# One core, adaLN with a Fourier mixer and an MLP: the modulation's first two vectors loaded scale first, the shift added inside the folds, and a planner that counts the half clock

## The chip, the core and the metric

The program runs on one core of one Trainium2 chip. The core has five engines that run their own instruction streams and meet through semaphores: TensorE (PE, matrix products; its weight loads are listed apart as PEld), VectorE (DVE), ScalarE (ACT), GpSimd (POOL) and SyncE (SP, which here only issues DMA transfers). Data lie in the DRAM of the device and in the core's SBUF (128 partitions); products land in PSUM, eight banks of 128 x 512 fp32 numbers. The metric is the device time of the whole program in microseconds (us). The kernel before the change takes 1337.07 us, the median of three runs (1335.74 to 1341.33).

## The reference

Sequence length 2048, width 1024, hidden width 3584, batch 1, all fp32. The core of it:

```python
x = A_x
mod = (_silu(c) @ w_mod).reshape(c.shape[0], 6, 1, -1)
sa, ca, ga, sb, cb, gb = (mod[:, 0], mod[:, 1], mod[:, 2], mod[:, 3], mod[:, 4], mod[:, 5])
h = _layernorm(x, axis=-1) * (1 + ca) + sa
x = x + ga * _A_ref(h, ...)      # real part of DFT_seq(DFT_hidden(h)), by four DFT matrices
h = _layernorm(x, axis=-1) * (1 + cb) + sb
x = x + gb * _B_ref(h, B_w1, B_b1, B_w2, B_b2)   # layernorm, w1 and b1, tanh gelu, w2 and b2
```

So there are two halves: a Fourier mixing of the modulated x, and an MLP on the modulated result. Six vectors of 1024 numbers, the modulation, come out of one product of silu(c) with the 1024 x 6144 matrix w_mod. The first two, the shift sa and the scale 1+ca, are needed at the start.

## The kernel before, in words

**Precision.** Products that need fp32 results run in fp16: each operand is scaled by a power of two and split into a high and a low half, and three products are summed (high x high, high x low, low x high).

**The front, up to about 305 us of the trace.** Four groups of work overlap there.

1. *Loads and the modulation.* SP issues the loads in an order written out in the code: rows of x (x0 to x15, 128 rows of 1024 each), a quarter of w1, and the first 2048 columns of w_mod (sa and ca together) as eight loads of 1 MB, one for each 128 rows k (`wm2(k)`). `mod_part(k)` (line 2604) multiplies silu(c) with each in fp32, four quarters of 512 columns, on 32 partitions each. When the last k is done, `row_max` (line 2615) and an all-reduce on POOL give the largest absolute value of sa and ca, `scales` makes a power of two of it, `rows_out` (2628) and `cols` (2633) turn the vectors into columns, and `cols_out` (2637 to 2645) writes `mcol` (scaled columns), `mneg` and `mbias`. All of it together is the task "mod".
2. *First layernorm and even/odd folds.* A cosine transform needs only sums and differences of mirrored columns, so the normalised x is folded. x comes in four groups bt = 0..3 of four tiles. For each group: statistics on DVE (line 2693) for bt 0 to 2 and on ACT for bt 3, the normalisation on ACT (2723 to 2727), transposes on PE (2740), then per pair of transposed blocks one ACT instruction with scale and shift (2753, task `lna`) and two DVE instructions (2757 and 2758, task `lnd`) that add and subtract the mirrored block. Groups 0 and 1 make class 0, groups 2 and 3 class 1. For each class `folds` then adds and subtracts further (2808 twice, 2814 twice, 2827 four times), and each of its two halves, called hop, is split by ACT (2833, high) and DVE (2835, low).
3. *Hidden and sequence transforms.* `hid` units (2.1 us each in the plan, line 3060) multiply the hops with DFT columns: class 0's products, then class 1's. Their results are split by ACT (2586) and DVE (2589). Eight blocks b = 0..7 of the sequence transform follow; in each, Q (3136) then P (3124) on PE, a copy on ACT (3140), and two DVE adds that form y (3145 and 3150, task `yev`).
4. *Second layernorm and z.* For each block: ga times y (3267), x added by a DMA, sums of squares on ACT (3241, 3615), cb and sb applied on DVE (3296, 3300), normalisation (3309); then the result is transposed (3490, `zT`), combined by unit products (3498), and split into seven sums z (3511 on ACT, 3538 on DVE) for the MLP's products. The z of blocks 4 to 7 are stored to DRAM by POOL (3530), behind which stand its other transfers (2183, 3271). Blocks 6 and 7 are held: their z is made later, during the main products.

Beside this, DVE and ACT split the first parts of w1 and w2 and the DFT matrices (2434, 2447, 2461, 2586, 2589), and the other modulation vectors are made row by row (2956, 2969).

**The main products.** gemm3 (line 3962) and gemm4 (line 4089), 2352 matmuls each, work by a scheme with seven products in place of eight. The first two groups of gemm3 need only z of blocks 0 to 3. They begin at about 275 us, and from about 305 us to the end PE runs them back to back.

**What sets the order.** A planner in the program's own Python: every piece of work is a `Task` with an engine, a cost in us, and the tasks it needs. Tasks wait in streams, each with an urgency `due` (smaller goes first). `pick_first` lets the engine that is free earliest take the most urgent task that can start. Costs, lags after a dependency (`LAGS`) and landing times (`LANDS`) are constants. The plan fixes the order in which each engine's instructions are written; on the chip each engine then runs its own in that order and waits where it must. `due_at(v)` says when the held blocks' z is made among the main products.

## Time and profile before

| | us |
|---|---|
| median of three runs | 1337.07 (1335.74 to 1341.33) |
| profiled execution | 1336.37 |
| its span, first to last instruction | 1334.6 |
| start of the first hidden product (line 3060) | 107.33 |
| start of the first main product (line 3962) | 274.91 |
| from where the main products run without a gap | 305.04 |
| last of PE's work | 1324.8 |
| mean granted TensorE clock | 0.964 |

PE is busy for 92% of the span, DVE for 79%, ACT for 56%, POOL for 19%. Over the main products PE is busy 1012.77 of 1019.80 us; before that it is busy 215.74 of 305 us. A "granted clock" of 0.5 means that the TensorE clock ran at half of full speed in that stretch. In a row of the timeline the bracket at the end gives how long the engine had been idle before that group of instructions and what ended the wait; in a table of windows each line is start:end, length, and the busy time of PE, PEld, DVE, ACT and POOL with the number of instructions, then the granted clock, the DMA engines' busy share and GB/s.

### The profile page before, as it was taken

Reading aid. Unit: us, or ns where it says so; the run is one execution under the profiler, and the core shown is the slowest. Engines: PE = TensorE matmul, PEld = TensorE weight load, DVE = VectorE, ACT = ScalarE, POOL = GpSimd, SP = SyncE. Lnnn points to the kernel's source line nnn. Section 1 sums busy time; section 2 is a strip of 40 time slices with the busy share of each in tenths; the row PEclk is TensorE's granted clock in tenths of the full one; section 3 lists DMA queues with packets and bytes.
Section 4 is the critical chain, followed back from the end, with each engine's and each line's share of the span. In section 5 each row is a group of like instructions: output and inputs, shape, how many; then the busy total and the mean of one; then the engine's idle time right before and its main releaser. Section 6 shows DMA issues by size and latency. Waiting matters only on the chain.

```text
span 1334.6 us, 16823 instructions
## 1 busy us (share of the span) xinstructions
...
## 2 busy tenths in 40 slices
...
GB/s 364 402 298 268 111 244 214 173 262 278 170 113 231 107 247 175 196 156 111 251 89 291 162 394 170 292 271 331 200 298 176 270 240 190 199 280 195 60 177 114
DMA packets 105704, 292.59 MB, mean 219 GB/s; under 512 B 13340, under 2 KB 13356, under 8 KB 103688
## 3 DMA queue, kind: packets, MB, share of 16 engines
...
## 4 chain that ended last, share of the span: by engine, by line
PE 69%; DVE 6%; issue 2%; ACT 2%; DMA 1%; POOL 0%; SPq 0%; DVEq 0%; POOLq 0%
PE ps L3962 34%; PE ps L4089 34%; DVE arena L2447 2%; DVE arena L4141 1%; ACT arena L2434 1%; DMA fw<-arena 1%; DVE arena L2461 1%; DVE arena L3538 0%; DVE arena L3988 0%; ACT arena L3981 0%; PE ps L3387 0%; ACT arena L3511 0%; DVE arena L3296 0%; DVE arena L3375 0%; DVE arena L4196 0%
## 5 line engine op out<-in xcount | busy, mean ns | idle before, releaser
L3962 PE MATMUL ps<-arena 128*128 128x512 f16 x2352 | 514.6, 381 | 7.8 <-DVE arena L3150 6.6
L4089 PE MATMUL ps<-arena 128*128 128x512 f16 x2352 | 511.7, 379 | 5.9 <-DVE arena L4141 5.4
L3962 PEld LDWEIGHTS <-arena 128*128 128x128 f16 x2352 | 231.0, 98 | 287.9 <-issue 13.2
L4089 PEld LDWEIGHTS <-arena 128*128 128x128 f16 x2352 | 230.0, 98 | 284.4 <-issue 7.6
L4141 DVE SCALAR_TENSOR_TENSOR arena<-ps,i4c,arena 128x1024 f32<-128x1024 f32 x179 | 229.2, 1280 | 79.5 <-PE ps L4089 78.3
L2434 ACT ACTIVATE arena<-arena,shc 128x512 f16<-128x512 f32 (+1 forms) x115 | 116.2, 1016 | 119.4 <-DVE arena L2461 67.0
L2447 DVE SCALAR_TENSOR_TENSOR arena<-arena,shc 128x512 f16<-128x512 f32 (+1 forms) x115 | 128.9, 1121 | 39.1 <-ACT arena L2434 38.9
L3846 ACT ACTIVATE arena<-arena 128x512 f32<-128x512 f32 (+4 forms) x159 | 97.3, 613 | 111.7 <-DVE arena L3855 91.1
L2461 DVE TENSOR_TENSOR arena<-arena 128x512 f32<-128x512 f32 (+1 forms) x196 | 149.4, 764 | 4.0
L3981 ACT ACTIVATE arena<-arena,b1s,i1c 128x512 f32<-128x512 f32 x78 | 63.4, 813 | 86.4 <-DVE arena L3988 86.4
L2434 ACT ACTIVATE arena<-arena,s1c 128x512 f16<-128x512 f32 (+1 forms) x70 | 60.6, 886 | 65.2 <-DVE arena L2461 33.5
L3855 DVE TENSOR_TENSOR arena<-arena 128x256 f32<-128x256 f32 x240 | 88.4, 419 | 3.6 <-DMA arena<-in_cre_dram 3.0
L3988 DVE TENSOR_TENSOR arena<-arena,ps 128x512 f32<-128x512 f32 x78 | 53.3, 684 | 43.2 <-PE ps L3962 41.9
L3627 POOL PARTITION_ALL_REDUCE sums<-sums x21 | 11.5, 552 | 373.3 <-DVE sums L3623 355.2
L2447 DVE SCALAR_TENSOR_TENSOR arena<-arena,s1c 128x512 f16<-128x512 f32 (+1 forms) x70 | 65.9, 960 | 10.0 <-ACT arena L2434 9.6
L3984 ACT ACTIVATE arena<-ps 128x512 f32<-128x512 f32 x78 | 45.9, 589 | 39.0 <-PE ps L3962 38.7
L2447 DVE SCALAR_TENSOR_TENSOR arena<-arena,s2c 128x1024 f16<-128x1024 f32 x49 | 61.7, 1279 | 2.9 <-ACT arena L2434 2.8
L2434 ACT ACTIVATE arena<-arena,s2c 128x1024 f16<-128x1024 f32 x49 | 54.7, 1137 | 2.7 <-DVE arena L2461 1.7
L3060 PE MATMUL ps<-arena 128*128 128x256 f16 (+5 forms) x297 | 47.0, 310 | 8.3 <-ACT arena L2833 3.2
L3615 ACT ACTIVATE ps<-arena 128x1024 f32<-128x1024 f32 x46 | 46.8, 1018 | 9.1 <-DMA arena<-in_w_dram 4.7
L3892 POOL DMA_DIRECT2D arena<-in_cim_dram x69 | 38.1, 558 | 54.6 <-ACT arena L3846 26.4
L2740 PE MATMUL ps<-ident,arena 128*128 128x128 f32 x128 | 23.3, 329 | 25.1 <-POOL arena L2901 14.7
...
## 6 DMA issues: line engine op xcount, KB each, us to landing
...
```

What stands on the lines that cost most here:

```text
L2434: act.activation(o[m][0], q(j), AF.Copy, **sc)
L2447: dve.scalar_tensor_tensor(o[m][1], q(j), scale, o[m][0], op0=ALU.mult, op1=ALU.subtract)
L2461: dve.tensor_tensor(q(d), q(a), q(b), op=op)
L3060: pe.matmul(PA(bp + o, (1, w), pn=m), l, r, start=i == 0, stop=i == len(mm_) - 1)
L3615: act.activation(junk, parts[j][0], AF.Square, accum_out=t[:, j : j + 1])
L3846: f = lambda: act.activation(v, v, AF.Square, accum_out=csum[0:pn, n : n + 1])
L3855: return lambda: dve.tensor_tensor(dst[0][:, o::2], src[0][:, o::2], dst[0][:, o::2], op=op)
L3962: pe.matmul(ps.rearrange("p (k t) -> p k t", k=4), w1at(g, m)[:, a, d * P : (d + 1) * P], zc(m)[:, b, :, d, :], start=(start and d == 0 an ...
L3981: act.activation(dst, src, AF.Gelu_apprx_tanh, scale=inv, bias=b1s[:, 2 * p + j : 2 * p + j + 1])
L3988: after_pe("dve", 0.6, lambda: dve.tensor_tensor(q, q, ps[b], op=ALU.add), kp[b])
L4089: pe.matmul(t[:, j], hidc[:, c_, m, a, k * P : (k + 1) * P], w2c[:, m, c_, w], start=(start and c_ == 0 and n == 0), stop=(c_ == 1 and n = ...
L4141: lambda: dve.scalar_tensor_tensor(dst, ps[b], inv, dst, op0=ALU.mult, op1=ALU.add), kp[b],
```

## The change

Four things are changed together. Line numbers from here on that belong to the changed program are some 80 to 110 higher than those of the kernel before.

**1. The two modulation vectors in two halves.** The eight 1 MB loads become sixteen of 0.5 MB: the scale half (ca) for all k before x8 to x11, the shift half (sa) behind them, into the same eight buffers (each waits for the scale half's product of its k). `mod_part`, `rows_out`, `cols` and `cols_out` run once for each half; the scale half ends in "moda", the shift half in "mod". The columns are no longer multiplied by the common power of two: the split into high and low (line 2833's and 2835's places) does that instead.

```diff
-    for i in range(4):
-        load_x(i)
+    def load_wm(h):
+        for k in range(8):
+            f = lambda k=k: sp.dma_start(wm2(k), wm[:, k, h * D : (h + 1) * D])
+            load(("wm", h, k), f, [] if h else [("mp", 1, k)])
...
-    for i in range(4, 8):
-        load_x(i)
-    for k in range(8):
-        load(("wm", k), lambda k=k: sp.dma_start(wm2(k), wm[:, k, 0 : 2 * D]), cost=2.75)
-    for i in range(8, 12):
-        load_x(i)
+    load_xs(1)
+    load_wm(1)
+    load_xs(2)
+    load_wm(0)
+    load_draw()
...
-    def cols_out():
-        dve.tensor_scalar(
-            mcol.rearrange("p a (b r) c -> p (a b) (r c)", b=2), PA(TB_, (32, 4), (128, 4)), sh, None, op0=ALU.mult
-        )
+    def cols_out(h):
+        dve.tensor_copy(mcol[:, h].rearrange("p (b r) c -> p b (r c)", b=2), PA(TB_ + 64 * h, (32, 2), (128, 4)))
+        if h:
+            dve.tensor_scalar(mneg, mcol[:, 1, 2:4], -1.0, None, op0=ALU.mult)
+            return
...
+        add("modr", "act", 0.66, lambda h=h: rows_out(h), [last_mp], ("rowc", h), 1.0)
+        add("modp", "pe", 0.6, lambda h=h: cols(h), [("rowc", h), *([] if h else ["vspec", "moda"])], ("cols", h), 1.0)
+        add("modm", "dve", 0.3 if h else 0.9, lambda h=h: cols_out(h), [("cols", h), *([] if h else ["sh"])], "moda" if h else "mod", 1.0)
```

**2. The shift of class 0 in the folds.** For class 0 `lna` multiplies by the scale alone and needs only "moda". The shift is constant along the sequence, so it is added after the first folds, in `s2_bias`: four instructions of 128 x 256, one of 128 x 1024 and two tiny ones in place of one `s2` of 128 x 2048. Class 1 stays as it was and needs "mod".

```diff
-                k1 = add("lna", "act", 0.78, lambda e=e, ba=ba, sc=sc, bi=bi: act.activation(
-                    e, bank(ba), AF.Identity, scale=sc, bias=bi), [ks[0], "mod"], None, 1.6)
+                if cls:
+                    f = lambda e=e, ba=ba, sc=sc, bi=bi: act.activation(e, bank(ba), AF.Identity, scale=sc, bias=bi)
+                else:
+                    f = lambda e=e, ba=ba, sc=sc: act.activation(e, bank(ba), AF.Copy, scale=sc)
+                k1 = add("lna", "act", 0.78, f, [ks[0], "mod" if cls else "moda"], None, 1.6)
...
-        k1 = add(f"fold{cls}", "dve", 2.4, lambda: s2(0, ALU.add), [k1], None, due)
+        def s2_bias():
+            for j in range(2):
+                for arr in range(2):
+                    o = FA(eo(j, arr, 0, 0), (1, 256))
+                    dve.scalar_tensor_tensor(
+                        o, o, mbias4[:, arr, j : j + 1], FA(eo(j, arr, 0, 512), (-1, 256)), op0=ALU.add, op1=ALU.add
+                    )
+            o = FA(eo(0, 2, 0, 0), (4 * AR, 2), (AR, 2), (1, 256))
+            dve.tensor_tensor(o, o, FA(eo(0, 2, 0, 512), (4 * AR, 2), (AR, 2), (-1, 256)), op=ALU.add)
+            o = [FA(eo(j, 0, 0, 0), (AR, 2), (256, 2)) for j in range(2)]
+            for j in range(2):
+                dve.tensor_tensor(o[j], o[j], medge[:, j], op=ALU.add)
+
+        if cls:
+            k1 = add(f"fold{cls}", "dve", 2.4, lambda: s2(0, ALU.add), [k1], None, due)
+        else:
+            k1 = add(f"fold{cls}", "dve", 3.0, s2_bias, [k1, "mod"], None, due)
...
-            h = add(f"foldh{cls}", "act", 2.0, lambda hi=hi, src=src: act.activation(hi, src, AF.Copy), [ka, *(([("n", 15), ("wrr", 5)] + [("cru", 6), ("cru", 7)] * loc) if cls else [("wrr", 2)])], None, due)
+            h = add(f"foldh{cls}", "act", 2.0, lambda hi=hi, src=src: act.activation(hi, src, AF.Copy, scale=sh), [ka, "mod", *(([("n", 15), ("wrr", 5)] + [("cru", 6), ("cru", 7)] * loc) if cls else [("wrr", 2)])], None, due)
             add(
-                f"foldl{cls}", "dve", 2.4, lambda hi=hi, lo=lo, src=src: dve.tensor_tensor(lo, src, hi, op=ALU.subtract),
+                f"foldl{cls}", "dve", 2.4, lambda hi=hi, lo=lo, src=src: dve.scalar_tensor_tensor(lo, src, sh, hi, op0=ALU.mult, op1=ALU.subtract),
```

**3. A plan with a half clock, and unused products.** In the front the planner now models the TensorE clock in windows of 3.41 us (`pe_run`): a window with little PE work makes a later one run at half speed. Where a planned PE task would start after a gap, and from 45 us of the plan on, `keep_warm` writes products of the identity matrix (128 x 128 fp16, 256 columns) into a PSUM bank that is free then. Nothing reads them. There are 129 of them in the changed program: 7 ahead of the last transposes of the layernorm, one among class 1's hidden products, and the others in groups of 3 to 23 from the sequence transform on.

```diff
+            if self.eng == "pe" and in_order[0]:
+                keep_warm(self, self.start())
             t = self.start() + self.cost
+            if self.eng == "pe" and in_order[0]:
+                t = pe_run(self.start(), self.cost, 0.7 if self.tag == "hidp" else 1.0)
...
+    TICK, PHASE = 3.4133, 0.0
+    pe_work, pe_state = {}, [0.5]
...
+    def pe_run(t, cost, weight):
+
+        while cost > 1e-9:
+            k = int((t - PHASE) // TICK) + 1
+            while len(pe_state) <= k:
+                w = pe_work.get(len(pe_state) - 1, 0.0) / TICK
+                n = len(pe_state)
+                up = w > 0.85 or min(pe_work.get(n - i, 0.0) for i in (1, 2, 3)) > 0.6 * TICK
+                pe_state.append(0.5 if w < 0.46 else 1.0 if up else pe_state[-1])
+            d = min(cost / pe_state[k], PHASE + k * TICK - t + 1e-6)
+            pe_work[k] = pe_work.get(k, 0.0) + weight * d
+            cost -= d * pe_state[k]
+            t += d
+            pe_spans.append((t - d, t))
+        return t
+
...
+    def keep_warm(task, start):
+
...
+        free = dict(spare)
+        if task.own:
+            free[task.own[0]] = max([0.0] + [done[d] + LAT for d in task.own[1] if d is not None])
+        b = min(free, key=lambda k: free[k])
+        idle = TICK - sum(e - max(s, start - TICK) for s, e in pe_spans)
+        n = int(min(start - max(clk["pe"], free[b]) - 0.3, idle - IDLE) / 0.11)
+        if n <= 0:
+            return
+        w = ident.bitcast(F16) if hasattr(ident, "bitcast") else ident[:, :].bitcast(F16)
+        for _ in range(n):
+            pe.matmul(PA(512 * b, (1, 256)), w[:, 0:P], w[:, 0 : 2 * P], start=True, stop=True)
+        clk["pe"] = pe_run(max(clk["pe"], free[b]), 0.11 * n, 1.0)
...
+    KEEP, IDLE = 45.0, 0.8
```

**4. Urgencies, costs and places.** A table `DUES` of 59 entries replaces the urgency of named streams, and some costs, lags and addresses change with it. The held blocks' z moves: its first transposes stand behind main product 972 instead of 696, those of the second behind 1716 instead of 1500. The steps' arithmetic stays the same.

```diff
+    DUES = {
+        ("cop0l", 58.0): 63.7, ("cop0l", 59.0): 60.5, ("cop1l", 61.0): 58.9, ("coph", 26.0): 40.3,
...
+    }
...
+            t.tag, t.due, t.lag = tag, DUES.get((stream, due), due), LAGS.get(f"{stream}l" if t.eng == "dma" else stream, LAGS.get(stream, LAT))
             streams.setdefault(f"st_{stream}" if t.eng == "st" else stream, deque()).append(t)
...
-    LAGS = {"w": 2.0, "rowl": 1.0, "crawl": 0.5, "row": 0.2, "rowp": 3.0, "ld": 0.5, "z": 1.0, "s": 0.5, "u": 0.3, "op": 0.4, "comb": 0.3, "ln": 0.2}
+    LAGS = {"w": 2.0, "rowl": 1.0, "crawl": 0.5, "row": 0.2, "rowp": 0.4, "ld": 0.5, "z": 1.0, "s": 0.5, "u": 0.3, "op": 0.4, "comb": 0.3, "ln": 0.2}
...
-        return due[3, 2] + 200.0 + 150.0 * v
+        return due[3, 2] + 150.0 + 180.0 * v
```

What this does to the order is seen in three places. **The first** is DVE between about 40 and 60 us of the trace, where the modulation's columns are made and the folds begin. Before (line 2615 is the largest value, 2637 to 2645 the columns, 2757 and 2758 the folds):

```order
L2447 SCALAR_TENSOR_TENSOR arena_65<-arena_65,s1c_171 128x2x512
L2615 TENSOR_REDUCE mx_121<-ps 128x1
L2619 TENSOR_SCALAR vspec_122<-ps,sel_123 128x2 x2
L2622 TENSOR_SCALAR m_4_109<-mx_121 128x1
...
L2637 TENSOR_SCALAR mcol_124<-ps,m_4_109 128x16
L2640 TENSOR_SCALAR msp_125<-ps,m_4_109 4x2
L2641 TENSOR_SCALAR mneg_126<-mcol_124 128x4
L2642 TENSOR_TENSOR mbias_127<-mcol_124 128x2
...
L2589 SCALAR_TENSOR_TENSOR arena_65<-arena_65 128x2x257
L2757 SCALAR_TENSOR_TENSOR arena_65<-ps,mneg_126,arena_65 128x512
L2758 SCALAR_TENSOR_TENSOR arena_65<-ps,mcol_124,arena_65 128x512
```

Now (2720 and 2722 write the columns, 2850 and 2851 are the folds, 2783 statistics, 2695 the largest value):

```order
L2720 COPY mcol_124<-ps 128x8
L2722 TENSOR_SCALAR mneg_126<-mcol_124 128x4
L2517 SCALAR_TENSOR_TENSOR arena_65<-arena_65,s1c_172 128x2x512
L2850 SCALAR_TENSOR_TENSOR arena_65<-ps,mneg_126,arena_65 128x512
L2851 SCALAR_TENSOR_TENSOR arena_65<-ps,mcol_124,arena_65 128x512
...
L2783 BN_STATS xst_22_165<-arena_65 128x6 x2
...
L2695 TENSOR_REDUCE mx_121<-ps 128x1
...
L2901 TENSOR_TENSOR arena_65<-arena_65 128x2x2x512 x2
L2907 TENSOR_TENSOR arena_65<-arena_65 128x8x256
L2699 TENSOR_SCALAR vspec_122<-ps,sel_123 128x2 x2
...
L2917 SCALAR_TENSOR_TENSOR arena_65<-arena_65,vspec_122 128x256 x4
```

The first fold stands right behind the scale's columns; all eight pairs of class 0, the statistics of group 2 and three of the large folds stand ahead of the columns of the shift.

**The second** is DVE around the last y of the sequence transform (3145 and 3150 before, 3256 and 3261 now; the rows between are ln2 of blocks 4 and 5 and the splits of z). Before:

```order
L3296 SCALAR_TENSOR_TENSOR arena_65<-arena_65,lns_25_167 128x1024
L3538 TENSOR_TENSOR arena_65<-ps,arena_65 128x2x512
L2673 RECIPROCAL lns_24_166<-lns_24_166 128x2
...
L3300 SCALAR_TENSOR_TENSOR arena_65,lns_24_166<-arena_65,lns_24_166 128x1024 x2
L3296 SCALAR_TENSOR_TENSOR arena_65<-arena_65,lns_25_167 128x1024
L3288 SCALAR_TENSOR_TENSOR csum_160<-csum_160 128x2
L3145 TENSOR_TENSOR arena_65<-ps,arena_65 128x2x256
L3150 TENSOR_TENSOR arena_65<-ps,arena_65 128x2x257
```

Now (3378 is what 3267 was, 3649 what 3538 was):

```order
L3649 TENSOR_TENSOR arena_65<-ps,arena_65 128x2x512
L2763 RECIPROCAL lns_24_167<-lns_24_167 128x2
...
L3418 SCALAR_TENSOR_TENSOR lns_24_167<-lns_24_167 128x2
L3378 SCALAR_TENSOR_TENSOR arena_65,lns_25_168<-arena_65 128x1024
L3399 SCALAR_TENSOR_TENSOR lns_25_168<-lns_25_168,csum_161 128x2
L3256 TENSOR_TENSOR arena_65<-ps,arena_65 128x2x256
L3649 TENSOR_TENSOR arena_65<-ps,arena_65 128x2x512
L3378 SCALAR_TENSOR_TENSOR arena_65,csum_161<-arena_65 128x1024
L3261 TENSOR_TENSOR arena_65<-ps,arena_65 128x2x257
```

The two passes of 3300 and the passes of 3296 no longer stand between the last two y; two large instructions now stand between the halves of the last y.

**The third** is POOL's queue of transfers at the end of the front (3530 before and 3641 now store z of block 4, then of block 5; 3271 and 3382 add a held block's row tile to the output; 3627 and 3738 are the all-reduce for the scale of w2). Before:

```order
L3530 DMA fzc_68<-arena_65 256x1x512
L2183 DMA out_dram<-arena_65,idxm_108 1024x1024
L3530 DMA fzc_72<-arena_65 256x1x512
L3530 DMA fzc_70<-arena_65 256x1x512
L3271 DMA out_dram<-arena_65 128x1024
L3530 DMA fzc_71<-arena_65 256x1x512
L3530 DMA fzc_73<-arena_65 256x1x512
L3530 DMA fzc_69<-arena_65 256x1x512
L3627 ISA sums_2032<-sums_2032 128x1
L3530 DMA fzc_67<-arena_65 256x1x512
```

Now:

```order
L3641 DMA fzc_71<-arena_65 256x1x512
L3382 DMA out_dram<-arena_65 128x1024
L3641 DMA fzc_73<-arena_65 256x1x512
L3641 DMA fzc_69<-arena_65 256x1x512
L2183 DMA out_dram<-arena_65,idxm_108 1024x1024
L3382 DMA out_dram<-arena_65 128x1024
L3641 DMA fzc_67<-arena_65 256x1x512
L3738 ISA sums_2182<-sums_2182 128x1
L3641 DMA fzc_68<-arena_65 256x1x512
```

All seven stores of block 4 are now issued ahead of the second held block's output transfers and ahead of the all-reduce. On PE, at the same place, 24 main products stand ahead of block 5's transposes before (12 of them ahead of block 4's); now it is 72 (12 and then 60), all behind block 4's transposes, ahead of which 25 of the unused products stand.

137 lines of the change are left out of this document (87 added, 50 removed), and 3 rows, old and new, of the table DUES.

## The prediction, made before the changed kernel was run

> **What bounds the kernel now.** I read the table by stretches first, then the timeline at each border of it, then the rows of single costs. The stretches end at the first product of the modulation's columns, the columns' end, the first hidden product, class 1's long run of hidden products, the last hidden result, the first main product, the point from which those run without a gap, and PE's end. Columns: start:end, length, busy PE, PEld, DVE, ACT, POOL, granted clock, DMA share, GB/s.
>
> ```profile
> 20.30:46.70 26.40, 18.00 (x89) 4.91 (x88) 11.21 (x34) 13.23 (x25) 3.73 (x7) 0.75 1.02 417
> 46.70:107.30 60.60, 39.68 (x206) 20.92 (x206) 55.43 (x85) 50.60 (x81) 0.35 (x1) 0.80 0.96 323
> 107.30:139.10 31.80, 25.37 (x200) 14.09 (x199) 29.07 (x33) 17.59 (x25) 1.71 (x2) 0.95 0.64 228
> 139.10:169.30 30.20, 28.32 (x138) 14.52 (x139) 19.01 (x27) 14.46 (x21) 1.26 (x4) 0.67 0.44 155
> 169.30:274.90 105.60, 80.37 (x480) 49.55 (x479) 93.41 (x170) 68.50 (x111) 30.88 (x29) 0.90 0.76 208
> 274.90:305.00 30.10, 22.02 (x96) 10.72 (x96) 15.83 (x38) 20.15 (x29) 9.50 (x12) 0.87 0.89 263
> 305.00:1324.80 1019.80, 1012.77 (x4701) 460.14 (x4699) 821.23 (x1185) 546.01 (x886) 200.38 (x293) 1.00 0.64 208
> ```
>
> From 305 us PE is busy 1012.77 of 1019.80 us at full clock, and none of the 4704 main products is removed. So a gain can only come from the front: the main products must run gapless from an earlier moment, or more of them must be done by then. In the front DVE is the fullest engine in three stretches (55.43 of 60.60, 29.07 of 31.80, 93.41 of 105.60 us), and PE the fullest while class 1's hidden products run (28.32 of 30.20, at a mean clock of 0.67). Ahead of that, DVE is idle for more than half of the time.
>
> **A. The scale half first.** DVE's rows around the columns, and the stretch ahead of them:
>
> ```profile
> 34.50:46.70 12.20, 7.42 (x33) 2.00 (x34) 3.47 (x15) 7.51 (x15) 1.37 (x3) 0.50 1.03 413
> 41.51 1.93 PE L2604 MATMUL ps<-arena,scol 128*32 128x512 f32 x8 [1.29 <-DMA arena<-in_wm_dram]
> 43.51 0.69 DVE L2615 TENSOR_REDUCE mx<-ps 128x1 f32<-128x512 f32 x1 [7.29 <-PE ps L2604]
> 46.12 0.23 DVE L2637 TENSOR_SCALAR mcol<-ps,m 128x16 f32<-128x16 f32 x1 [0.65 <-PE ps L2634]
> 46.65 0.78 ACT L2753 ACTIVATE arena<-ps,mbias,mcol 128x512 f32<-128x512 f32 x1 [0.19 <-DVE mbias L2642]
> ```
>
> The wait goes back to the loads of w_mod, which flow at 417 GB/s with the DMA engines full. The scale half is 4.2 MB less than both, so its last product starts 4.2 MB / 417 GB/s = 10 us earlier, near 31.5 us. That product is half as long (1.0 us), and from its end to the columns it took 46.1 - 43.4 = 2.7 us: columns near 34.5 to 35. DVE is idle for 12.20 - 3.47 = 8.7 us between there and 46.7; the folds and the statistics of group 2, whose x now loads ahead of the shift half, can use it. Their prices:
>
> ```profile
> L2693 DVE BATCH_NORM_STATS2 xst<-arena 128x6 f32<-128x512 f32 x24 | 15.0, 669 | 5.7 <-DMA arena<-in_x_dram 5.7
> L2757 DVE SCALAR_TENSOR_TENSOR arena<-ps,mneg,arena 128x512 f32<-128x512 f32 x16 | 11.9, 744 | 1.6 <-ACT arena L2753 1.5
> L2814 DVE TENSOR_TENSOR arena<-arena 128x2048 f32<-128x2048 f32 x4 | 9.2, 2290 | 0.1
> L2827 DVE TENSOR_TENSOR arena<-arena 128x1024 f32<-128x1024 f32 x6 | 7.4, 1226 | 0.2
> L2792 DVE TENSOR_TENSOR arena<-arena 64x256 f32<-64x256 f32 x2 | 0.8, 418 | 0.1
> ```
>
> Eight fold pairs of class 0 are 16 x 0.75 = 12 us and four tiles' statistics 8 x 0.67 = 5.4 us, so there is more work than gap. The shift in the folds costs four instructions of 256 columns at 0.42, one of 1024 at 1.23 and two tiny ones at 0.15, 3.2 us, in place of 2.29: +0.9. Copying and negating columns twice adds some 0.7 (four instructions like the 0.15 to 0.23 of line 2637's kind). Of the 5.17 us (60.60 - 55.43) that DVE idles between 46.7 and 107.3, I count one more as closed. A = 8.7 + 1 - 1.6 = **8 us** earlier for the first hidden product. Low end 3 (half of the gap used, since ACT's normalisation and scaling feed the folds and ACT is itself busy 50.60 of 60.60 us), high end 12 (all of both gaps, 13.9 - 1.6). The product of the shift half comes last but is wanted only behind three large folds of 2.29 us, so I let it wait for nothing. The scale in the split and the 16 smaller loads move the same bytes: nothing.
>
> **B. Class 1's hidden products and the half clock.** The first of these rows is class 0, at full clock; of the other runs two are at half:
>
> ```profile
> 107.33 18.85 PE L3060 MATMUL ps<-arena 128*128 128x257 f16 x147
> 139.10 11.26 PE L3060 MATMUL ps<-arena 128*128 128x257 f16 x49 [2.78 <-DVE arena L2835]
> 152.11 5.64 PE L3060 MATMUL ps<-arena 128*128 128x257 f16 x45
> 159.63 8.37 PE L3060 MATMUL ps<-arena 128*128 128x257 f16 x36 [1.88 <-DVE arena L2589]
> 140.00:142.00 2.00, 2.00 (x10) 0.50 0.00 0
> 144.00:146.00 2.00, 2.00 (x11) 0.50 0.00 0
> 150.00:152.00 2.00, 2.00 (x7) 1.00 0.00 0
> ```
>
> 0.125 us each at full clock (5.64 / 45), 0.23 at half (11.26 / 49). At full clock the 49 and the 36 would take 10.6 in place of 19.6 us: 9 us at most. The changed order runs class 1's products with the whole rows ahead of them, but PE's gap between the classes (DVE makes the hop, 29.07 of 31.80 us busy) stays, and only one unused product stands there. So the clock will still be lost at the start: I take half, 4.5 us, and both ends, 0 and 9. Ahead of the first y DVE gets 1.2 us of ga and w1 work that stood behind it. B = 4.5 - 1.2 = **3.3 us** (-1.2 to 7.8).
>
> These rows show 11 us at half clock with PE busy 2.00 of 2.00. The Trainium skill, TensorE: Matmul & The Clock Gate, Part 1, says that one busy window of some 3.4 us brings the full clock back; the trace disagrees here. By its rule the two runs would have lost 1.7 us each, the clock could give back at most 3.4, and the sum below would be at least 1 us smaller.
>
> **C. From the first y to the last.** DVE bounds this stretch (93.41 of 105.60 us), so instructions that leave it count in full:
>
> ```profile
> L3267 DVE SCALAR_TENSOR_TENSOR arena<-arena 128x1024 f32<-128x1024 f32 x14 | 17.1, 1219 | 0.1
> L3296 DVE SCALAR_TENSOR_TENSOR arena<-arena,lns 128x1024 f32<-128x1024 f32 x12 | 15.2, 1279 | 0.9 <-ACT arena L3241 0.9
> 273.57 0.69 DVE L3145 TENSOR_TENSOR arena<-ps,arena 128x512 f32<-128x512 f32 x1
> 274.91 4.96 PE L3962 MATMUL ps<-arena 128*128 128x512 f16 x12 [6.61 <-DVE arena L3150]
> ```
>
> Between the first and the last y the changed order has one ga (1.22) and two cb passes (1.28) less: 3.8 us. C = **4 us** (0 if ACT or the transfers of x hold it, 5 with the gaps between). Against it, two large instructions (a split of z and a ga, 1.22 each) now stand between the halves of the last y, ahead of what takes PE's banks: **-2.4** (0 if PE is busy with block 4's transposes until then).
>
> **D. The last z.** Before, PE has its gaps in this stretch (22.02 of 30.10 us) while the chain through POOL's queue ends:
>
> ```profile
> 293.38 0.95 POOL L3271 DMA_DIRECT2D out_dram<-arena  x1 [4.33 <-issue]
> 301.77 1.02 ACT L3511 ACTIVATE arena<-ps 128x1024 f16<-128x1024 f32 x1 [5.43 <-DMA fzc<-arena]
> 301.93 0.45 POOL L3627 PARTITION_ALL_REDUCE sums<-sums  x1
> 302.42 0.15 DVE L3631 TENSOR_SCALAR sums<-sums 128x1 f32<-128x1 f32 x1 [5.89 <-POOL sums L3627]
> 305.04 5.34 PE L3962 MATMUL ps<-arena 128*128 128x512 f16 x24
> ```
>
> ACT waits 5.43 us for a z store of block 4 that stands behind a held block's output transfer. By 305.04 36 main products are done (three groups of 12). One costs 5.34 / 24 = 0.22 us, so the start that counts is 305.04 - 36 x 0.22 = 297.1, 22.2 us behind the last y. Now all of block 4's stores go ahead of that transfer, and 72 main products stand ahead of block 5's transposes where 24 stood, so PE can fill most of its 8.1 us of gaps. I take half, D = **4 us**, ends 0 and 10 (all gaps, and 2 of the 5.43).
>
> The unused products cost nothing in this sum: they stand in gaps of PE (33 us idle of 135.7 from 169.3 to 305). If that cover is gone, the third rival gives the price. The held z move inside stretches in which PE is busy 99%; their stalls there are 7 us in all, so moving them is 0, give or take 3. The end behind PE's last product (1334.6 - 1324.8 = 9.8 us) stays.
>
> Sum: 8 + 3.3 + 4 - 2.4 + 4 = 16.9 us off the profiled execution of 1336.4: 1319.5. The profiled execution is 0.7 below the median of the runs, so 1320 stands for the median. The low ends (3, -1.2, 0, -2.4, 0) add up to -0.6, the high ones (12, 7.8, 5, 0, 10) to 34.8.
>
> **Rivals.** 1. *More, 1307.* The engines stay in step as planned: A 11, B 7, C 4, D 8, no delay of the last y, 30 us. For it: a plan that knows the half clock puts DVE's work where it is wanted. Against: all terms must hold, and ACT and DMA are untouched.
>
> 2. *No difference, 1333.* The front is fed by the DMA engines (share 1.02, then 0.96 until 107.3), and class 1 can't start before x12 to x15 and its first splits. If class 1's hop comes when it did, A is spent in a longer gap between the classes, and what is left is B's clock or D, 0 to 6 us. Against: x12 to x15 load some 2 MB earlier, and DVE, not a load, ends the waits at 139.10 and 159.63.
>
> 3. *Slower, 1344.* 121 unused products stand between class 1's products and the last z. Their price is not in the trace; bounds are half a main product's 0.22, 0.11 us, and 0.23, the hidden product at half clock with as many columns. At 0.23 they are 28 us. PE's busy 102.4 of 135.7 us becomes 130, PE is the bound of the sequence transform, and the work behind them comes late: if 25 of the 28 us lie ahead of work that is ready, 17 of gain turn into 8 of loss. It decides from the point where more than 60% of the 28 us delay PE's real work. For it: PE's queue is in order, and an earlier y on the chip than in the plan finds the unused products ahead of it. Against: most stand where the plan has PE waiting for DVE.
>
> **How the numbers follow.** Forecast (a gain between 7 and 25 us) 0.70, more 0.10, no difference 0.11, slower 0.09. A measurement of this kernel tells about 0.5%, 6.7 us, from no change: faster by more than that 0.80, within it 0.11, slower 0.09. The range: 1304 takes in rival 1 and nearly all high ends, 1335 the low ends and rival 2; it leaves out rival 3 and the edges.
>
> **What would show it.** A: line 2850's first fold near 36 us, the first hidden product (3169) near 99; wrong if folds wait for ACT or POOL. B: class 1's run at clock 1.0 and its last result near 156 to 158. C and D: the last y near 260, the gapless run 17 us earlier. If the first hidden product is early and class 1's are not, rival 2 was right; if the unused products read 0.2 us or more and PE is busy throughout 160 to 290, rival 3. The gapless stretch from there on must keep its length; a longer one would make the whole sum wrong.

## The result: 0.9% slower

| | before | changed |
|---|---|---|
| median (range, runs) | 1339.39 (1335.74 to 1341.33, 6) | 1351.75 (1347.52 to 1353.21, 6) |
| ratio, 95% interval | | 1.0093 [1.0074, 1.0112] |
| span of the profiled execution | 1334.6 | 1350.1 |
| first hidden product | 107.3 | 109.4 |
| last hidden result | 168.0 | 169.8 |
| first y, last y | 180.1, 274.9 | 185.8, 272.4 |
| main product 36 done | 301.2 | 284.5 |
| product 300, 1500, 2200 done | 362.2, 626.6, 780.5 | 365.3, 632.1, 798.1 |
| last main product done | 1324.8 | 1342.4 |

The first hidden product is taken at its start, all other moments at their ends; main products are counted in the order in which PE ran them, 4704 in all. Line numbers of the changed kernel: hidden products 3169, the halves of y 3256 and 3261, gemm3 4073, gemm4 4200, their evacuations 4095 (ScalarE's copies) and 4252.

The table by stretches of the changed kernel, cut at the same events (columns as in the prediction: start:end, length, busy PE, PEld, DVE, ACT, POOL, granted clock, DMA share, GB/s):

```profile
20.30:46.70 26.40, 21.23 (x88) 7.04 (x84) 19.18 (x41) 15.87 (x28) 1.82 (x3) 0.87 1.03 407
46.70:109.40 62.70, 38.20 (x203) 18.49 (x202) 46.61 (x84) 46.22 (x76) 2.25 (x5) 0.76 0.83 277
109.40:185.80 76.40, 62.85 (x442) 35.76 (x441) 61.70 (x87) 40.22 (x55) 5.19 (x12) 0.96 0.65 224
185.80:272.40 86.60, 76.10 (x524) 52.27 (x524) 77.94 (x143) 63.07 (x100) 23.68 (x21) 0.98 0.71 193
272.40:365.30 92.90, 78.74 (x351) 35.66 (x350) 57.88 (x87) 57.98 (x81) 18.76 (x22) 0.93 0.72 227
365.30:798.10 432.80, 417.81 (x1933) 190.07 (x1932) 391.02 (x555) 266.22 (x351) 28.44 (x40) 0.99 0.55 183
```

and of the kernel before, for the stretches that the prediction's table cuts otherwise:

```profile
107.30:180.10 72.80, 64.48 (x418) 34.93 (x417) 57.94 (x82) 37.68 (x52) 5.68 (x11) 0.84 0.54 188
180.10:274.90 94.80, 69.57 (x400) 43.23 (x398) 83.55 (x147) 62.88 (x104) 28.16 (x24) 0.90 0.78 213
274.90:362.20 87.30, 79.22 (x361) 36.64 (x361) 60.87 (x93) 60.82 (x80) 15.33 (x19) 0.95 0.72 232
362.20:780.50 418.30, 414.47 (x1933) 189.47 (x1932) 383.76 (x549) 264.27 (x346) 27.33 (x40) 1.00 0.55 185
```

Read side by side: DVE works more ahead of 46.7 (19.18 in place of 11.21 us), as predicted, but the stretch behind it has a hole (46.61 of 62.70, it was 55.43 of 60.60) and the first hidden product comes 2.1 us *later*. From there to the first y another 3.6 us are lost. The stretch from the first y to the last is 8.2 us shorter. Behind the last y everything won is lost: 5.6 us up to product 300, and 14.5 us (432.80 against 418.30) in products 300 to 2200, where PE ran almost without a gap before. Behind product 2200 both need the same 544.3 us to the last one, and the changed kernel ends 2.1 us sooner after it: 2.1 + 3.6 - 8.2 + 5.6 + 14.5 - 2.1 = 15.5, the difference of the spans. (The medians differ by 12.4 us; the profiled execution of the kernel before is 3.0 us faster than its median.) How far one trace can be trusted is seen in e10 and e11 below: their front is that of the kernel before, instruction for instruction, and they have the first hidden product at 107.7 and 107.1 us, but the last y at 275.0 and 277.4 and product 300 at 364.0 and 366.3. So the 14.5 us and the 2.1 at the first hidden product stand clear of this spread, and the 5.6 us up to product 300 may be 2 us less.

### Three places in the trace

**The row copy waits for two small instructions.** DVE, ACT and PE of the changed kernel, in order of time (2720 copies the scale's columns, 2901 and 2907 are the large folds, 2699 is the small work on the modulation row, 2710 copies the row out of its bank, 2715 turns it into columns):

```profile
36.38 0.11 DVE L2720 COPY mcol<-ps 128x8 f32<-128x8 f32 x1
37.80 0.74 DVE L2850 SCALAR_TENSOR_TENSOR arena<-ps,mneg,arena 128x512 f32<-128x512 f32 x1
51.65 0.69 DVE L2695 TENSOR_REDUCE mx<-ps 128x1 f32<-128x512 f32 x1 [0.95 <-PE ps L2685]
56.76 4.62 DVE L2901 TENSOR_TENSOR arena<-arena 128x2048 f32<-128x2048 f32 x2
61.42 2.29 DVE L2907 TENSOR_TENSOR arena<-arena 128x2048 f32<-128x2048 f32 x1
63.63 0.34 DVE L2699 TENSOR_SCALAR vspec<-ps,sel 128x2 f32<-128x2 f32 x2
64.00 0.38 ACT L2710 ACTIVATE arena<-ps 64x255 f32<-64x255 f32 x1 [9.77 <-DVE vspec L2699]
64.43 0.91 PE L2715 MATMUL ps<-ident,arena 97*128 97x97 f32 x4 [9.62 <-ACT arena L2710]
68.93 0.68 DVE L2670 SCALAR_TENSOR_TENSOR arena<-arena 1x512 f16<-1x512 f32 x1 [3.79 <-ACT arena L2667]
```

The shift's row is ready at 51.6, but 2699 stands behind 6.9 us of folds on DVE. ACT's copy reads the same bank. ACT is free for it from 54.2, and it starts at 64.00, directly behind 2699. Everything else in ACT's queue stands behind it for 9.77 us, and DVE then waits for ACT.

**The held output transfer lands late.** The chain of waits (start, duration, what) and then PE's rows:

```profile
302.66 10.31 DMA out_dram<-arena
312.98 0.03 issue
313.01 5.05 DMA arena<-in_w_dram
318.06 0.02 issue
318.08 1.15 ACT arena L2504
319.23 0.49 ACT arena L4405
```

```profile
319.77 15.36 PE L4073 MATMUL ps<-arena 128*128 128x512 f16 x60 [6.75 <-ACT arena L4405]
338.85 6.33 PE L4073 MATMUL ps<-arena 128*128 128x512 f16 x15 [3.73 <-ACT arena L4095]
```

The second held block's output transfer is issued at 302.66, behind block 4's stores (the transfer of line 3271 in the prediction's row was issued at 293.38). The loads of w2 wait for its place in the SBUF, ACT's split 2504 waits for the loads, and the copy 4405, which frees PE's bank, stands behind that split.

**Main products 1873 and after.**

```profile
721.08 14.39 PE L4073 MATMUL ps<-arena 128*128 128x512 f16 x60 [6.65 <-ACT arena L4095]
743.63 16.74 PE L4200 MATMUL ps<-arena 128*128 128x512 f16 x69 [2.98 <-DVE arena L4252]
```

Before, PE's longest wait in products 300 to 2200 was 1.79 us; now it waits 6.65 and 2.98 us there, and products 1500 to 2000 take 122.9 us in place of 110.7. The copy that ends the first of these waits is the 31st of line 4095. Counted in the traces, ACT has run 41 splits of w2 (line 2504 with the scale `s2c`) ahead of it; in the kernel before it was 40, ahead of the same copy.

### The profile page after: what moved, and what is told of

It is laid out like the page before. It is cut to its first block, busy times and chain, and to the rows that moved or that the text cites. A ratio compares the mean times of both kernels' runs of the same rounds, so it can differ in the third digit from the quotient of the medians.

```text
span 1350.1 us, 17107 instructions
## 1 busy us (share of the span) xinstructions
PE 1238.6 (92%) x6042; PEld 584.4 (43%) x6042; DVE 1060.3 (79%) x1611; ACT 742.0 (55%) x1196; POOL 251.9 (19%) x383
## 4 chain that ended last, share of the span: by engine, by line
PE 67%; DVE 12%; ACT 7%; DMA 7%; issue 5%; SPq 1%; POOL 1%; DVEq 0%; POOLq 0%; ACTq 0%
PE ps L4200 34%; PE ps L4073 29%; DVE arena L2517 3%; DMA arena<-in_wm_dram 2%; ACT arena L2504 2%; DMA out_dram<-arena 2%; DVE arena L4252 1%; DVE arena L2531 1%; DMA arena<-in_w_dram 1%; DVE arena L2670 1%; DVE arena L3649 1%; ACT arena L2667 1%; DMA frow_cb<-arena 1%; PE ps L2685 1%; DVE arena L3411 1%
## 5 line engine op out<-in xcount | busy, mean ns | idle before, releaser
L4073 PE MATMUL ps<-arena 128*128 128x512 f16 x2352 | 518.0, 382 | 21.9 <-ACT arena L4095 12.1
L4200 PEld LDWEIGHTS <-arena 128*128 128x128 f16 x2352 | 230.4, 98 | 289.2 <-issue 11.7
L2504 ACT ACTIVATE arena<-arena,shc 128x512 f16<-128x512 f32 (+1 forms) x115 | 116.2, 1016 | 117.8 <-DVE arena L2531 65.8
L2517 DVE SCALAR_TENSOR_TENSOR arena<-arena,s1c 128x512 f16<-128x512 f32 (+1 forms) x70 | 66.2, 960 | 16.2 <-ACT arena L2504 16.1
L2517 DVE SCALAR_TENSOR_TENSOR arena<-arena,s2c 128x1024 f16<-128x1024 f32 x49 | 61.6, 1280 | 12.9 <-ACT arena L2504 12.8
L4003 POOL DMA_DIRECT2D arena<-in_cre_dram x69 | 38.9, 576 | 38.7 <-ACT arena L3957 18.7
L3169 PE MATMUL ps<-arena 128*128 128x256 f16 (+5 forms) x297 | 39.7, 277 | 4.1 <-DVE arena L2670 3.5
```

The costliest lines, as they stand in the source:

```text
L2504: act.activation(o[m][0], q(j), AF.Copy, **sc)
L2517: dve.scalar_tensor_tensor(o[m][1], q(j), scale, o[m][0], op0=ALU.mult, op1=ALU.subtract)
L4003: return lambda t: gp.dma_start(t[0:pn], v)
L4073: pe.matmul(ps.rearrange("p (k t) -> p k t", k=4), w1at(g, m)[:, a, d * P : (d + 1) * P], zc(m)[:, b, :, d, :], start=(start and d == 0 an ...
L4200: pe.matmul(t[:, j], hidc[:, c_, m, a, k * P : (k + 1) * P], w2c[:, m, c_, w], start=(start and c_ == 0 and n == 0), stop=(c_ == 1 and n = ...
```

## The experiments

All ratios are to the kernel before, run beside them; its median there was 1337.35 for e1 to e4, 1337.03 for e5 to e8, 1337.62 for e9 to e11 and 1338.16 for e12 to e14.

### e1: without the unused products

```diff
-            pe.matmul(PA(512 * b, (1, 256)), w[:, 0:P], w[:, 0 : 2 * P], start=True, stop=True)
+            pass
```

> The changed kernel with the 129 unused products left out; every other instruction stays in its place. Theory (the loss comes from three new waits: ACT behind the shift's columns in the front, w2's loads behind the held blocks' output stores near 313 us, and the moved second held z near 715 us): the unused products cost and save little, 1348 to 1355. Rival (they stand ahead of ready work on PE, as the third rival of the prediction had it): at least 6 us faster than the change, 1345 or less. Second rival (they keep the clock up and so are worth something): 1356 or more, with more half clock between 170 and 290.

Measured: 1351.85 (1350.74 to 1352.97), 1.0105 [1.0064, 1.0147], the same as with them. In the changed kernel they cost PE 16.6 us:

```profile
L2313 PE MATMUL ps<-ident 128*128 128x256 f16 x129 | 16.6, 274 | 1.7 <-ACT arena L3251 1.4 <-DVE arena L3261 0.2
```

They seem to raise the clock: without them half clock lasts 54.5 us between 45 and 280 us, with them 40.9, and 41.8 to 48.1 in e2, e3 and e13, which have them too; but one front varies as much from trace to trace (60.9 to 74.6 us in the kernel before, e10 and e11). Neither shows in the time. That fits a front in which the other engines, DVE above all, set the pace; it wasn't tested apart. So the unused products aren't the loss (and no gain).

### e2: the held z where it stood

```diff
-        return due[3, 2] + 150.0 + 180.0 * v
+        return due[3, 2] + 200.0 + 150.0 * v
```

> The changed kernel with the held blocks' z back at the old place in the plan (200 + 150 v in place of 150 + 180 v). Theory: the 11 us that the change loses between main products 2000 and 2200 come from that place, and most of them go: 1340 to 1345, and no wait of 6.7 us on line 4095 near 715. Rival (they are late w2 work carried over from the stall near 313 us): within 3 us of the change, 1349 to 1355.

Measured: 1349.64 (1347.35 to 1352.28), 1.0085 [1.0055, 1.0114]. The stall that it was to remove grew:

```profile
723.16 14.75 PE L4073 MATMUL ps<-arena 128*128 128x512 f16 x60 [11.47 <-ACT arena L4095]
```

The place of the held z alone isn't the cause. Here 42 splits of w2 stand ahead of the copy that product 1873 waits for, one more than in the changed kernel.

### e3: the held output transfers ahead of the last four z4 stores

```diff
-        ("ln1", 232.0): 235.2,
+        ("ln1", 232.0): 190.0,
...
-    store("z", (b, n), lambda dst=dst, v=v: gp.dma_start(dst, v), ("z", b, m), tag=tag)
+    store("z", (b, n), lambda dst=dst, v=v: gp.dma_start(dst, v), ("z", b, m),
+          *([("st", "xo", 2 * q + e) for q in HELD for e in range(2)] if b == 4 and n >= 3 else []), tag=tag)
```

> The changed kernel with the held blocks' output transfers issued ahead of the last four z stores of block 4 (a dependency of those stores, and block 7's ga pass made urgent); nearly all else keeps its place. Theory: w2's loads follow the last output transfer, which goes out some 8 us earlier; the wait of 6.75 us near 313 and the half clock behind it go, 1335 to 1343. Rival (the DMA engines are full there, so the loads land as late in any order): 1348 to 1355.

Measured: 1343.49 (1340.16 to 1346.0), 1.0042 [1.0022, 1.0061]: 8.3 us off the changed kernel. The 6.75 us at product 133 is gone (product 300 at 361.0 in place of 365.3). The stall of 6.64 us before product 1873 stays. So the late transfer is shown to be one loss. (The edit also moves some twenty instructions each on DVE and ACT, nearly all between 275 and 350 us; PE's order is the same.)

### e4: the halves and the shift in the folds alone

The old costs, lags and held place; no clock in the plan, no unused products, no searched urgencies; the new loads, halves and folds stay. The core of it:

```diff
-    KEEP, IDLE = 45.0, 0.8
+    KEEP, IDLE = None, 0.8
...
-                t = pe_run(self.start(), self.cost, 0.7 if self.tag == "hidp" else 1.0)
+                pass
...
-            t.tag, t.due, t.lag = tag, DUES.get((stream, due), due), ...
+            t.tag, t.due, t.lag = tag, due, ...
...
-        add("seqp", "pe", 2.68 if tp else 2.9, p_mm, ...
+        add("seqp", "pe", 3.0, p_mm, ...
```

> The two halves and the shift in the folds alone: no clock in the plan, no unused products, the old urgencies, costs, lags and places. Theory (in the front the shift's columns stand behind three large folds, so ACT idles and the first hidden product is no earlier; the later losses belong to the plan's numbers): 1334 to 1342, the first hidden product at 105 to 110. Rival (the halves gain their 8 us as predicted and the plan's numbers lose it all): 1325 to 1331, the first hidden product near 99.

Measured: 1341.09 (1337.89 to 1347.79), 1.0032 [1.001, 1.0054]. The halves alone gain nothing; their first hidden product is at 109.7 as well. Their main products run as in the kernel before (1500 to 2000 in 110.7 us, no wait above 1.78 us in products 300 to 2200). So the third loss comes from the plan's numbers, and the first is there with the halves alone.

### e5: vspec right behind the maximum

```diff
     def row_max():
         dve.tensor_reduce(mx, PA(VB, (1, 512)), axis=AX.X, op=ALU.max, apply_absolute_value=True)
-
-    def row_spec():
         for h in range(2):
             dve.tensor_scalar(vspec[:, 2 * h : 2 * h + 2], PA(VB, (256, 2)), sel[:, h : h + 1], None, op0=ALU.mult)
+
+    def row_spec(): pass
```

> The changed kernel with one edit: the two small VectorE instructions on the modulation row (vspec) are issued right behind the row's maximum, ahead of the three large folds and not behind them; every other instruction keeps its place. Theory that VectorE sets the pace up to product 2200, and that the 9.77 us which ScalarE's row copy waited for vspec is what the changed kernel loses between 46.7 us and the first hidden product: that wait falls below 2 us, VectorE's idle time from 46.7 us to the first hidden product falls from 16.1 to about 7, the first hidden product starts near 100 (109.4), and product 2200 starts 6 to 10 us earlier than in the changed kernel: 1342 to 1346 of its 1351.75. Rival, that the wait is only moved (the row copy is late from something else, the fold or the maximum): the first hidden product stays within 3 us of 109.4 and the time within 3 us of 1351.75.

Measured: 1342.62 (1340.4 to 1343.85), 1.0042 [1.0029, 1.0054]: 9.1 us off the changed kernel. ACT's copy no longer waits:

```profile
53.56 0.69 ACT L2846 ACTIVATE arena<-ps,mcol 128x512 f32<-128x512 f32 x1 [0.19 <-PE ps L2830]
54.14 0.36 ACT L2710 ACTIVATE arena<-ps 64x255 f32<-64x255 f32 x1
```

DVE's idle time from 46.7 us to the first hidden product falls from 16.1 to 7.7 us, that product starts at 101.6 (109.4; before 107.3), and the time of product 2200 falls by 8.5. DVE and ACT keep all other instructions in their order, and PE keeps its own. The theory held in place and size.

### e6: both repairs

The edits of e3 and e5 together.

> Both repairs: vspec right behind the row's maximum, and the held output transfers ahead of the last four z4 stores (which alone gave 1343.49). If the two losses add, since both are idle time of VectorE ahead of product 2200: 1333 to 1338, about as fast as the kernel before (1337.35). Rival, that one hides the other (what the front wins is lost again at the stalls near products 1500 to 2000, as product 300 at 361 us already was there): 1341 to 1344.

Measured: 1335.79 (1333.98 to 1339.0), 0.9987 [0.9974, 1.0], no difference from the kernel before. The two losses add (9.1 + 8.3 expected, 16.0 measured). But the last y is at 264.2, 10.7 us earlier than before, and the time isn't. What is left:

```profile
264.20:351.70 87.50, 76.93 (x351) 35.29 (x350) 57.44 (x87) 57.74 (x80) 17.94 (x22) 0.94 0.75 242
351.70:782.60 430.90, 417.26 (x1933) 189.80 (x1932) 390.82 (x555) 266.35 (x351) 28.53 (x40) 0.99 0.55 183
```

Product 300 is 10.5 us earlier than before, and products 300 to 2200 take 12.6 us longer, with 390.82 us of DVE work in place of 383.76.

### e7: the edit of e5 on the halves alone

> The halves and the shift in the folds alone (the old costs and urgencies, no unused products; alone it took 1341.09), with vspec right behind the row's maximum. Theory that the late vspec also costs this version its front: the first hidden product starts near 100 and not at 109.7, the time falls by 6 to 10 us to 1331 to 1335, faster than the kernel before. Rival, that here something else holds the row back: within 3 us of 1341.

Measured: 1341.76 (1339.5 to 1346.62), 1.0034 [1.0016, 1.0051], no gain over e4. The theory missed: in this order the maximum itself stands behind the three folds (it starts at 62.13), and vspec stood right behind it already, so the edit moves nothing. ACT's wait stays:

```profile
63.16 0.38 ACT L2710 ACTIVATE arena<-ps 64x255 f32<-64x255 f32 x1 [10.41 <-DVE vspec L2697]
```

### e8: without the searched urgencies

```diff
-            t.tag, t.due, t.lag = tag, DUES.get((stream, due), due), ...
+            t.tag, t.due, t.lag = tag, due, ...
```

> The changed kernel without its table of searched urgencies; planner costs, halves, clock and unused products as they are. If the urgencies cause the loss in products 1500 to 2000 (stalls of 6.65 and 2.98 us near 721 and 744 us, each followed by half clock; the version without planner numbers has none): those stalls are gone and products 1500 to 2000 take 110 us in place of 123. If the loss comes from VectorE's backlog whatever the order: a stall of 3 us or more stays between 700 and 760 us. For the time as a whole, with the tail of the output transfer changed too: 1338 to 1352.

Measured: 1352.1 (1349.38 to 1353.68), 1.0107 [1.0088, 1.0126]. The stall before product 1873 is there to the hundredth (6.64 us), products 1500 to 2000 take 120.6. The searched urgencies neither cause the loss nor gain anything in the time; without them the last y is at 284.2 in place of 272.4, and two thirds of that difference are gone by product 300 (369.3 and 365.3).

### e9: another order of the main products

On the kernel of e6, one cost of the plan put back:

```diff
-        add("seqp", "pe", 2.68 if tp else 2.9, p_mm, ...
+        add("seqp", "pe", 3.0, p_mm, ...
```

> Both repairs as in the run that took 1335.79, and one planner cost put back (3.0 us in place of 2.68 and 2.9 for a shift product), which moves little ahead of product 0 but gives the main products another order. In the 31st copy of ScalarE behind the main products (the one that product 1873 waits for), the order so far had this many w2 splits more ahead of it than the kernel before: none in the kernel before and in the halves alone (PE's stall there 0.9 us or less), one in the changed kernel and in five variants of it (6.64 or 6.65 us each time), two with the held place put back (11.47 us). Here it has one fewer than the kernel before. Theory that ScalarE's order there sets the stall: the stall near product 1873 and the half clock behind it are gone, products 1500 to 2000 take 110 to 112 us and not 121, and the time is 1324 to 1329, 0.6 to 1 % faster than the kernel before. Rival, that VectorE has fallen behind by then in every order that starts the main products early: a stall of 5 us or more stays, 1333 to 1338.

Measured: 1353.24 (1350.49 to 1354.57), 1.0108 [1.0087, 1.013]. The theory missed the time by 24 us. The wait before product 1873 went (1.16 us are left, with 39 splits of w2 ahead of the copy), as its order foretold, but others came in its place:

```profile
711.11 7.93 PE L4073 MATMUL ps<-arena 128*128 128x512 f16 x36 [1.16 <-ACT arena L4095]
724.34 6.80 PE L4073 MATMUL ps<-arena 128*128 128x512 f16 x24 [5.30 <-ACT arena L4095]
...
819.44 10.93 PE L4200 MATMUL ps<-arena 128*128 128x512 f16 x42 [8.39 <-DVE arena L4252]
```

So the order decides where PE waits, and one cost, changed by 0.1 to 0.3 us in a task of the front, is worth 17 us through it. DVE has less work in products 300 to 2200 than in e6 (384.9 us, from 390.8), and the stretch is longer all the same (433.9 us, from 430.9).

### e10 and e11: more work for one engine

On the kernel before, 56 extra instructions on DVE, or 48 main products run twice:

```diff
+                if 1 <= v <= 4: dve.tensor_reduce(mx, ident, axis=AX.X, op=ALU.max)
```

```diff
-                    for n, (a, w) in enumerate(PASSES):
+                    for n, (a, w) in enumerate(PASSES[:1] * (start and c_ == 0 and 1 <= v <= 4) + PASSES):
```

> The kernel before with 56 extra VectorE instructions, each a maximum over 128 columns, one behind each evacuation of the second layer's products 588 to 1764; about 0.2 us each, 11 us together; TensorE's work and all orders unchanged. Theory that VectorE sets the pace until product 2200: 6 to 11 us slower, 1343 to 1348, with new stalls of TensorE there. Rival, the prediction's premise that TensorE's gapless stretch sets it and VectorE's gaps take up extra work: at most 3 us slower, and VectorE's idle time there is smaller by the added work.

> The kernel before with 48 products of the same stretch run twice (the first of a bank, overwritten by its second run), 0.215 us each, 10.3 us together; VectorE's work unchanged. If TensorE's stretch sets the pace: 9 to 11 us slower, 1346 to 1348. If VectorE sets it: TensorE's extra work lies in waits it would have had anyway and the time grows by less than 4 us.

Measured: e10 1347.83 (1344.13 to 1350.55), 1.0072 [1.0047, 1.0097]; e11 1349.3 (1343.61 to 1351.12), 1.0076 [1.005, 1.0102]; 10.2 and 11.7 us slower than the kernel before. Products 300 to 2200, first of e10, then of e11 (with the 48 doubled ones):

```profile
364.00:789.40 425.40, 416.69 (x1933) 189.37 (x1932) 393.40 (x605) 263.86 (x346) 27.57 (x40) 1.00 0.54 182
```

```profile
366.30:793.60 427.30, 424.44 (x1981) 194.23 (x1980) 385.16 (x549) 264.17 (x346) 28.04 (x40) 1.00 0.54 182
```

DVE's busy time grows by 9.6 us there (393.40 - 383.76) and the stretch by 7.1; PE's by 10.0 and the stretch by 9.0. Neither theory is right alone: PE's added work shows nearly in full, and of the work added to DVE, which is 92% full there, three quarters show as well. That it is DVE's fullness, and not the place of the added instructions right behind the evacuations that free PE's banks, isn't shown: they stood at no other place. In their traces the rest of the loss lies ahead of product 300 (at 364.0 and 366.3, from 362.2), where the programs don't differ.

### e12: both repairs, and the main products in the order of before

```diff
-        return due[3, 2] + 150.0 + 180.0 * v
+        return due[3, 2] + 200.0 + 150.0 * v
...
-    t = clk["pe"]
+    clk["pe"] += 12; t = clk["pe"]
```

> Both repairs (1335.79 alone), the held z back at 200 + 150 v, and the planner told at the start of the main phase that TensorE is 12 us later than it computed: from the third copy of ScalarE on, its order behind the main products is then that of the kernel before, while all that stands ahead of product 0 stays as in the kernel with both repairs. Theory that the order in the main products, and not the amount of VectorE's work, made products 1500 to 2000 take 121 us in place of 111: no stall above 2 us between products 300 and 2200, products 1500 to 2000 in 110 to 112 us, product 2200 near 772 (782.6) and 1323 to 1328 us in all, about 0.9 % faster than the kernel before. Rival, that VectorE owes the same work and gives the loss back elsewhere: product 2200 not ahead of 779, 1332 to 1338.

Measured: 1331.0 (1330.49 to 1333.43), 0.9944 [0.9927, 0.996]: faster than the kernel before, by 0.56%, and 4.8 us faster than e6. The time lies between the two ranges. Its two stretches behind the last y:

```profile
264.97:359.70 94.73, 77.98 (x351) 35.74 (x350) 64.69 (x95) 61.77 (x86) 18.96 (x23) 0.91 0.79 255
359.70:778.10 418.40, 414.56 (x1934) 189.51 (x1932) 383.39 (x547) 262.95 (x344) 27.62 (x40) 1.00 0.54 182
```

Products 300 to 2200 are back at the length of before (418.40; 1500 to 2000 in 110.7), as the theory has it. But 7.2 us more pass ahead of product 300 than in e6, as the rival has it, and the likely reason stands in the same rows: DVE has 64.69 us of work there in place of 57.44. The two effects are 12.5 and 8.0 us, and 4.5 are left. The wait that took the loss is on PE at 334.44, and ACT's queue at that moment shows how:

```profile
334.44 14.93 PE L4073 MATMUL ps<-arena 128*128 128x512 f16 x60 [10.61 <-ACT arena L4095]
```

```profile
321.49 1.15 ACT L2504 ACTIVATE arena<-arena,shc 128x1024 f16<-128x1024 f32 x1 [2.01 <-DVE arena L2531]
324.71 2.91 ACT L2504 ACTIVATE arena<-arena,shc 128x512 f16<-128x512 f32 x3 [2.08 <-DVE arena L2531]
...
330.59 1.15 ACT L2504 ACTIVATE arena<-arena,shc 128x1024 f16<-128x1024 f32 x1 [0.74 <-DVE arena L2531]
331.72 2.19 ACT L2504 ACTIVATE arena<-arena,s2c 128x1024 f16<-128x1024 f32 x2
333.82 0.57 ACT L4095 ACTIVATE arena<-ps 128x512 f32<-128x512 f32 x1
```

The copy that frees the bank (4095) stands behind splits (2504) that wait for DVE's sums (2531).

### e13: the order of the main products alone

The edit of e12 with 10 us on the changed kernel without the two repairs.

> The changed kernel with the third repair alone: the held z back at 200 + 150 v and TensorE planned 10 us later at the start of the main phase, so that the order of the main products is that of the kernel before from the third copy on; the front and the output transfer's place are as in the changed kernel. Theory of three separate losses: its share is 10 to 12 us, 1339 to 1343. Rival, that the stall only moves: 1347 to 1352.

Measured: 1342.54 (1340.83 to 1344.19), 1.0028 [1.0014, 1.0042]: 9.2 us off the changed kernel, products 1500 to 2000 in 110.7 us. So this is the third loss. Products 300 to 2200 are 14.5 us shorter than in the changed kernel, and product 300 comes 5.3 us later (370.6), as it does in e12 against e6. The three repairs are worth 9.1, 8.3 and 9.2 us alone, 26.6 in sum, and 20.8 together (e12): they overlap in part.

### e14: the halves alone with the maximum ahead of the folds

```diff
-        k1 = add(f"fold{cls}", "dve", 2.4, lambda: s1(0, ALU.add), d1, None, due)
+        k1 = add(f"fold{cls}", "dve", 2.4, lambda: s1(0, ALU.add), d1 if cls else ["vspec", ("rowc", 0), *d1], None, due)
```

(with the edit of e5, on the kernel of e4)

> The halves alone with the maximum, vspec and the row copy planned ahead of the three large folds (where vspec went behind the maximum alone, the maximum itself still stood behind the folds, and nothing was won: 1341.76). Theory that the shift half must be wanted ahead of those folds: ScalarE's wait of 10.4 us goes, the first hidden product starts at 100 to 104 and not 109.3, and since the main order is that of the kernel before the gain is kept: 1331 to 1336. Rival, that the folds put off by this make the hidden products as late: hidden products from 107 on, 1338 to 1343.

Measured: 1346.19 (1344.23 to 1348.01), 1.0054 [1.0035, 1.0072], slower than e4. The rival held, and more: the new tie changed the plan of the whole front. The shift products end at 60.5 (53.4 in e4), the large folds start at 65.1 (55.3 in e7), the first hidden product at 118.4. Whether the halves gain by themselves stays open: in e5 the first hidden product comes 5.7 us earlier than before, but there the new costs and urgencies work beside them, and no run has these without the halves.

## Why the prediction was wrong

The prediction said 1320 (1304 to 1335), faster; the kernel is 0.9% slower. Step by step:

**A, 8 us earlier for the first hidden product.** The first part held: the scale's columns came at 36.4 (34.5 to 35 predicted), the first fold at 37.80 (near 36), and DVE's idle time from 20.3 to 46.7 us fell by 8.0 us (8.7). The step that failed is the sentence "The product of the shift half comes last but is wanted only behind three large folds of 2.29 us, so I let it wait for nothing". It looked at when the result is *used* and not at what waits *in the queues* for it: DVE's two small instructions behind the folds, ACT's copy behind those, and the rest of ACT's queue behind the copy. That cost 9.77 us on ACT, and e5 gives it back: 101.6, 5.7 us earlier than before, between A's low end 3 and its 8.

**B, 3.3 us.** The clock did what was forecast: with the unused products and the new order, half clock between 100 and 185 us fell from 23.9 to 6.8 in these two traces, and class 1's products took 26.1 us from their hop to the last result in place of 28.9. But the stretch ahead of them, from the first hidden product to that hop, grew from 31.8 to 34.3, with DVE 30.02 of its 34.30 us busy. And behind them, from the last hidden result to the first y, it now takes 16.0 us in place of 12.1: PE ran without a gap there before, now it waits for a split of DVE (2670), which has more to do. Before, then the changed kernel, then PE's wait in it:

```profile
168.00:180.10 12.10, 12.10 (x84) 6.78 (x85) 10.49 (x25) 6.89 (x11) 2.71 (x5) 0.91 0.56 185
169.80:185.80 16.00, 13.03 (x93) 7.57 (x93) 15.36 (x32) 7.96 (x13) 4.45 (x10) 1.00 0.93 316
172.50 2.76 PE L3246 MATMUL ps<-arena 128*128 128x512 f16 x12 [2.69 <-DVE arena L2670]
```

So B came out at -3.6 (2.8 - 2.5 - 3.9). The term that failed is the 1.2 us for DVE: its work from the first hidden product to the first y grew by 3.8 us (61.70 from 57.94). And the clock's term should have been near 0, since PE's faster products only reach DVE's splits sooner: in e2, whose front has the same instructions, half clock lasts 13.7 us there, class 1's products end 2.3 us later behind their hop, and the first y comes as long after the first hidden product as in the changed kernel (76.7 and 76.4 us). What a better order of DVE would give wasn't tried.

**C, 4 - 2.4 us.** Undersized: from the first y to the last 8.2 us less where 1.6 was forecast, with DVE's work there down by 5.6 us, from 83.55 to 77.94. The two instructions between the halves of the last y are in the trace (the first half starts at 268.49, the second at 271.74; before, the two starts lay 0.60 us apart) and cost 2.65 us, about what was set.

**D, 4 us, and its low end 0.** The sign was wrong: the sum left out a wait. The prediction saw that block 4's stores now go ahead of the held output transfer and counted only what gets earlier. What got later is that transfer, and with it the SBUF place that w2's loads need, ACT's split of w2 and the copy behind it. PE did start its main products earlier (36 of them done at 284.5 in place of 301.2), and then stood. From the last y to product 300 it became 5.6 us longer; e3 wins back 8.3 of the whole.

**The premise, "The gapless stretch from there on must keep its length".** It didn't, and the prediction named this as what would make the whole sum wrong: 418.30 became 432.80. Its rows showed PE busy 1012.77 of 1019.80 us; they also showed DVE busy 821.23, and the prediction made nothing of that. As a mean to the end of the program it is 81%; in products 300 to 2200 DVE is 92% full (383.76 of 418.30), and in e10 three quarters of the work added to it there appear in the time.

The step of the sum that stood for this is "The held z move inside stretches in which PE is busy 99%; their stalls there are 7 us in all, so moving them is 0, give or take 3". It priced the move by the stalls of the order before, not by those that a new order makes, and the sum had no term for what the other new costs do to that order. Restoring the order gives back 9.2 us (e13), moving the held z back alone nothing that counts (e2).

The order, which the plan computes from its numbers, sets how much DVE work stands behind product 300: 390.5 to 391.5 us in the changed kernel, e1 to e3, e5, e6 and e8, and 383 to 384 with the order of before (e4, e7, e12 to e14). An early start of PE doesn't set it: e8 starts its main products 12 us later than the kernel before and has 390.5, e12 starts them 7 us earlier and has 383.4. The order also sets which copy of ACT stands behind which splits: ahead of the copy for product 1873 there are 40 splits of w2 in every kernel without that stall but e9, 41 in all those that wait 6.64 or 6.65 us, 42 in e2 with its 11.47 and 39 in e9, which stalls elsewhere. How the 14.5 us divide between DVE's work and the place of ACT's copies stays open.

**The rivals.** The third said slower, 1344, by the unused products. The direction came true by other mechanisms, which is luck; e1 refutes that one, and "The unused products cost nothing in this sum" holds. The second said that class 1's hop comes when it did and that A is spent in front of it: in e5, where A's wait is gone, the first hidden product is 5.7 us early and that hop 2.1 us (137.0, from 139.0), so more than half of A did go there. With that wait gone the last y comes 7.0 us earlier than before (e5), with the other repair too 10.7 (e6), where the first three terms had 12.9.

One piece of bookkeeping, not a cause, sums this up. In e1 to e8 and e12 to e14 DVE's busy time up to product 2200 is 666 to 668 us (before 665.6, changed 667.1), so product 2200 comes at that time plus DVE's idle time up to there (114.9 before, 131.1 changed, 116.2 in e6, 111.7 in e12). Among these kernels one that starts PE earlier has product 2200 earlier only if DVE's idle time got smaller. The change put 8.0 us of work into DVE's first gap, and 24 us of idle time arose elsewhere.
